# Denominators' transfers and first-layer stores on GpSimd's queue, values loaded last, the first layer a unit later, and another order of the last layer's left factors

## The chip, the cores and the metric

One core of a Trainium2 chip runs the whole program. Its engines are TensorE (PE, the matmuls; PEld is its weight loads), VectorE (DVE), ScalarE (ACT), GpSimd (POOL) and SyncE (SP, which here only issues transfers). Each engine takes its instructions strictly in order. The metric is the device time of one execution in microseconds: 926.24 us before, the median of three runs (923.36 to 926.26).

## The reference

A linear attention and two feed-forward layers, on 4 batches x 576 tokens and 8 heads of 64:

```python
proj = x @ w_phi;  proj -= max(abs(proj), axis=-1)
phi(x) = concat([exp(proj), exp(-proj)])             # 256 features, for q and for k
kv = k_p^T @ v;  z = sum_s k_p
attn = (q_p @ kv) / (q_p @ z + 1e-6)                 # numerators by denominators
h = max(attn @ w1, attn @ w2, attn @ w3)             # 2304 x 768, first layer
y = h @ w_out                                        # 2304 x 512, second layer
g = relu(y @ w_in) + alpha * min(y @ w_in, 0)        # 2304 x 2048, third layer
out = g @ w_out2                                     # 2304 x 512, last layer
```

## The kernel before

Matmuls run in a rounded 32-bit format. To keep accuracy a value x is split into a rounded part (line 68, ACT) and the rest (line 74, a subtraction, mostly on DVE), and a product is taken as three products of parts (`three`). A float32 matmul, used in the first two batches of the attention, is recorded as two.

**Attention.** The loop over `pairs` takes two heads at a time, 16 pairs, 4 to a batch. `load_pair` loads keys (k), values (v), the last 64 tokens of both (t) and queries (q), a pair ahead. `keys` projects (pj), takes the maximum (line 204, DVE), exponentiates on ACT and sums into kvp; `queries`, which runs a pair later, projects, transposes (pt), exponentiates and multiplies by kv, which leaves numerators and denominators in `nd` (line 335, ACT). The 18 pieces of w1, w2, w3 arrive as 64-bit floats (`fetch`, line 173) and are rebuilt on DVE and ACT (`split_w123`) in the first eight pairs.

**The denominators.** At the end of `queries` two small transfers spread the denominators over the partitions (dc, line 366), one moves the second head's numerators (line 367), DVE adds the epsilon and takes reciprocals (368, 369), one transfer writes them to HBM (r_d, line 371), and four read them back, broadcast, into two tiles xr (line 378). A product (line 380), a rounding and a subtraction make the first layer's input (xh, xl). For batch 0 these three run on POOL, later on DVE and ACT. All the transfers stand in SP's queue, between the loads and most of the first layer's stores.

**First layer.** A unit (`layer1`) is 36 matmuls for 288 tokens x 128 outputs: three sums (`p_814`, `p_827`, `p_840` for the first unit), each over four pairs' tiles. Its maximum goes to h_d (line 417; in the last batch from POOL). Units stand three to a pair behind the attention of the next batch, moved by `LAG`. They need all four pairs of their batch.

**Second and third layer.** `load_h` reads h_d back through tiles borrowed from several pools, and the second layer's results (yo, two buffers shared with ho) are stored from ACT's queue and read back by `load_y`. `convert` spreads the rebuilding of later weights over the units. The third layer stores g from POOL (line 628).

**Last layer.** `left` makes, for each half of a block of 256 tokens, seven left factors (a Strassen scheme, seven products in place of eight): four sums and differences s (lines 593 to 596), and for each factor a rounding on ACT and a subtraction, in turn on DVE and POOL. A half is 84 matmuls (line 656). The factors are made one half ahead of their use; DVE adds the results (668, 679).

The order within each engine's queue is laid down when the program is built: a scheduler places instructions by the order of the code and the priorities given there (`tc.high_priority`), so that an edit also moves instructions that it doesn't name.

Of the kernel before, what the change touches and what calls it, by code (L numbers as in the profile page):

```python
# [10 lines left out]
F32 = mybir.dt.float32  # L11
# [22 lines left out]
CHUNKS = ((0, 2 * P), (2 * P, S - 2 * P))  # L34
EPS = 1e-6
XBUFS = (6, 6)
LAG = 1
PLAIN = 5
CONVERT_IN = (2, 1, 2, 1, 3, 3, 3, 3)
SOON, NOW, LATER, LAST = 400, 1000, -100, -200  # L40
# [11 lines left out]
def tile_kernel(ctx: ExitStack, tc: tile.TileContext, qT, kT, tails, v, w_phi, w1, w2, w3, w_out, w_in, w_out2, alpha, out):  # L52
# [82 lines left out]
    def load_pair(pair):  # L135

        odd = pair[1] % 2
        tags = ["xh", "rv", "rt", "xl"] if plain(pair) else ["raw", "rv", "rt", "raw"]
        if plain_kv(pair):
            tags[1] = ("vl", "vh")[odd]  # L140
        shapes = ([P, SM], [P, 5, 3, D], [P, 2 * ST], [P, SM])
        for what, tag, shape, src in zip("kvtq", tags, shapes, (kT, v, tails, qT)):
            t = ap.tile(shape, F32, tag=tag, bufs=2 if tag in ("raw", "xh", "xl") else 1, name=what)
            nc.sync.dma_start(t, src[pair])
            raws[pair, what] = t

    def plain(pair):
        return pair[0] * NPAIR + pair[1] < PLAIN

    def plain_kv(pair):  # L150
        return pair[0] < 2
# [161 lines left out]
    def queries(pair):  # L313

        parts = ("q",) if plain_kv(pair) else ("qh", "ql")
        qf = []
        for n, (o, w) in enumerate(CHUNKS):
            qf.append([])
            for x in parts:
                tag = f"qh{n}" if x != "ql" and pair[1] % 2 * len(x) != 1 else f"ql{n}"  # L320
                qf[n].append(ap.tile([P, 2, 2, w], F32 if plain_kv(pair) else F32R, tag=tag, bufs=1, name=x))
        nd = [ap.tile([P, S], F32, tag="nd", bufs=3, name="nd") for _ in range(2)]

        def num(n):
# [12 lines left out]
        def tail():  # L337
            yield 2, (0,), tail_of[pair]

        for g, tiles, pp in chain(project_queries(pair), tail()):  # L340
            o, w = (0, 2 * P, SM)[g], ST if g == 2 else 2 * P
            pt = bank("pn" if pair[0] == 0 and g == 1 else "pt", 1, "pt")
            for i in range(len(tiles)):
                for h in range(2):
                    c = h * len(tiles) * P + i * P
                    nc.tensor.transpose(pt[:, c : c + P], pp[:, 2 * i + h], ident)  # L346
            n = min(g, 1)
            dst = [t[:, :, :, o - CHUNKS[n][0] : o - CHUNKS[n][0] + w] for t in qf[n]]
            if plain_kv(pair):
                e = dst[0]  # L350
            else:
                e = ap.tile([P, 2, 2, 256], F32, tag="qe", bufs=2, name="qe")[:, :, :, :w]
            pv = pt[:, : 256 * len(tiles)].rearrange("p (h s) -> p h s", h=2)[:, :, -w:]
            A.activation(e[:, :, 0], pv, AF.Exp)
            A.activation(e[:, :, 1], pv, AF.Exp, scale=-1.0)
            if not plain_kv(pair):
                (hi_dve if g == 1 else hi_act)(dst[0], e)
                sub(V, dst[1], e, dst[0])
            yield
            if g != 1:  # L360
                num(n)
        yield
        dc = ap.tile([P, S // D], F32, tag="dc", bufs=2, name="dc")
        for h in range(2):
            dr = D * (1 - h)
            nc.sync.dma_start(dc[h * D : (h + 1) * D], nd[h][dr : dr + 1].rearrange("a (p n) -> a p n", p=D))
        nc.sync.dma_start(nd[0][D:], nd[1][D:])
        V.tensor_scalar(dc, dc, EPS, None, op0=ALU.add)
        V.reciprocal(dc, dc)
        rows = r_d[pair[0], pair[1]]  # L370
        nc.sync.dma_start(rows.rearrange("h (p n) -> (h p) n", p=D), dc)
        res = []
        for c in range(2):
            cs = slice(c * CH, (c + 1) * CH)
            xr = raw_tile()
            for h in range(2):
                r = slice(h * D, (h + 1) * D)
                nc.sync.dma_start(xr[r], rows[h : h + 1, cs].to_broadcast([D, CH]))
            e = G if pair[0] == 0 else V
            e.tensor_tensor(xr, nd[0][:, cs], xr, op=ALU.mult)  # L380
            xh, xl = x_tiles(c)
            if pair[0] == 0:
                G.tensor_copy(xh, xr)  # L383
            else:
# [13 lines left out]
    def layer1(b, c, f, x, w, spread=False):  # L398
        pw = []
        for j in range(3):  # L400
            if spread:
                p = bank(("pn", "pt", "kv")[j], 1, "p1")
            else:
                p = bank("p1", 3, "p1")
            ops = []
            for k in range(KT):
                ks = slice(k * P, (k + 1) * P)
                ops += three(w[j][:, 0, ks], w[j][:, 1, ks], *x[k][c])
            products(p[:, :CH], ops)
            pw.append(p)  # L410
        s1 = xp.tile([P, CH], F32, tag="s1", bufs=2, name="s1")
        A.activation(s1, pw[0][:, :CH], AF.Copy)
        V.tensor_tensor(s1, pw[1][:, :CH], s1, op=ALU.max)
        ho = xp.tile([P, CH], F32, tag="ho", bufs=2, name="ho")
        V.tensor_tensor(ho, pw[2][:, :CH], s1, op=ALU.max)  # L415
        o = b * S + c * CH
        (nc.gpsimd if b == B - 1 else nc.sync).dma_start(h_d[f, :, o : o + CH], ho)  # L417

    pairs = [(b, pr) for b in range(B) for pr in range(NPAIR)]
    xs = {b: [] for b in range(B)}  # L420
# [94 lines left out]

    def load_h(c, k):
        hh, hl = x_tiles(max(c % 2, k // XBUFS[0]))
        pool, tag, bufs = ((xp, "xr", 3), (xp, "xr", 3), (xp, "s1", 2), (gp, "neg", 2))[(2 * c + k) % 4]
        if c == 0:
            pool, tag, bufs = xp, "xr", 3  # L520
        hr = pool.tile([P, CH], F32, tag=tag, bufs=bufs, name="hr")
        nc.sync.dma_start(hr, h_d[k, :, c * CH : (c + 1) * CH])
        hi_act(hh, hr)
        sub(V, hl, hr, hh)
        hs[c, k] = (hh, hl)
# [22 lines left out]
    for c in range(2 * B):  # L548
        t0 = c * CH
        p2 = [bank(*ab, "p2") for ab in SETS[c % 2]]  # L550
        if c + 1 < 2 * B:
            for k in range(NF1):
                load_h(c + 1, k)
        for m in range(KT):
            ms = slice(m * P, (m + 1) * P)
            ops = []
            for k in range(NF1):
                ops += three(wo[k][:, 0, ms], wo[k][:, 1, ms], *hs[c, k])
            products(p2[m][:, :CH], ops)
            yo = xp.tile([P, CH], F32, tag="ho", bufs=2, name="yo")  # L560
            A.activation(yo, p2[m][:, :CH], AF.Copy)
            nc.scalar.dma_start(y_d[m, :, t0 : t0 + CH], yo)
        convert(2)
# [18 lines left out]
    def left(block, half):  # L582

        ready[block, half] = res = {}
        a = []
        for kh in range(2):
            t = ap4.tile([P, 4, 2 * T], F32, tag="a", bufs=4, name="a")
            r = slice(kh * 8 + half * 4, kh * 8 + half * 4 + 4)
            nc.sync.dma_start(t, g_d[r, :, block * 2 * T : (block + 1) * 2 * T].rearrange("f p n -> p f n"))
            a.append(t)  # L590
        (a00, a10), (a01, a11) = ((t[:, :, :T], t[:, :, T:]) for t in a)
        s1, s2, s3, s4 = (ap4.tile([P, 4, T], F32, tag="s", bufs=4, name="s") for _ in range(4))
        V.tensor_tensor(s3, a00, a10, op=ALU.subtract)
        V.tensor_tensor(s1, a10, a11, op=ALU.add)
        V.tensor_tensor(s2, s1, a00, op=ALU.subtract)
        V.tensor_tensor(s4, a01, s2, op=ALU.subtract)  # L596
# [140 lines left out]
```

## Time and profile before

| | |
|---|---|
| median of three runs | 926.24 us (923.36 to 926.26) |
| the profiled execution | 925.09 us, of which its span 923.3 us |
| PE busy | 899.8 us, 97% |
| DVE busy | 642.5 us, 70% |
| ACT busy | 468.2 us, 51% |
| POOL busy | 173.5 us, 19% |

The profile is one execution. Times in its rows are from the span's start. A row of the windows gives each engine's busy time in a stretch and, behind an x, its instructions; PE's busy time contains matmuls that wait in its pipeline, so that the count of matmuls of one kind in 20 us says more than the busy share. A row of the timeline ends with the idle time of the engine before it and what ended it. "SPq" is SP's queue: a row there is an issue, not the transfer's own time.

### The profile page before, as it was taken

To read this page: it belongs to the slowest core of one execution; us is meant where nothing else is said; L and a number is where in the kernel's file an instruction comes from. 1 tells how busy PE (TensorE), PEld (TensorE's weight loads), DVE (VectorE), ACT (ScalarE), POOL (GpSimd) and SP (SyncE) were. 2 spreads that over 40 slices of the span, in tenths; PEclk is the share of its full clock that TensorE was granted. 3 is DMA by queue.
4 is the path that set the end of the run, shared out by engine and by line. 5 is a ranking of instruction groups with operands and counts; after the bars stand their busy time and mean duration, and the time that the engine had idled before them with its cause. 6 is when DMAs were issued, how large, how long until landed. Compare 5 with 4: busy or idle time off the path is not lost.

```text
span 923.3 us, 18029 instructions
## 1 busy us (share of the span) xinstructions
PE 899.8 (97%) x6689; PEld 876.6 (95%) x6689; DVE 642.5 (70%) x1239; ACT 468.2 (51%) x1084; POOL 173.5 (19%) x221
## 2 busy tenths in 40 slices
PE   8987999999999999999999999999999998999998
PEld 7866899999999999999999999999999998999998
DVE  6998556788887632889889294447443598878881
ACT  5867556777777521444466363335333353444440
POOL 0032100000000000001000023333333363444440
PEclk9999999999999999999999999999999999999999
DMA  9664323222331112766678555445542345443421
GB/s 318 195 193 143 84 59 81 74 80 82 104 95 44 31 58 65 225 184 213 203 231 248 185 171 167 131 147 175 193 149 100 111 116 156 135 141 116 138 69 46
DMA packets 83159, 125.98 MB, mean 136 GB/s; under 512 B 14208, under 2 KB 61952, under 8 KB 83072
## 3 DMA queue, kind: packets, MB, share of 16 engines
q1 hardware_dynamic: 71744, 99.47, 36.4%
q0 software_dynamic: 6720, 20.65, 6.2%
q10 hardware_dynamic: 4608, 4.72, 1.5%
q8 instruction: 52, 0.85, 0.4%
q14 instruction: 35, 0.29, 0.1%
HBM read 86.91 MB, written 35.46 MB: 133 GB/s over the span
## 4 chain that ended last, share of the span: by engine, by line
PE 73%; DVE 11%; DMA 8%; issue 3%; ACT 2%; SPq 0%; POOL 0%; ACTq 0%; DVEq 0%; POOLq 0%
PE p L253 43%; PE acc L656 12%; PE kvp L284 6%; PE pn L253 5%; PE pj L253 5%; DVE o L74 2%; DMA st<-in_w_out 2%; DMA y_d<-yo 2%; PE pt L346 2%; DMA hr<-h_d 1%; DVE wt L87 1%; DVE wt L89 1%; ACT o L68 1%; DVE xl L74 1%; DVE s L596 1%
## 5 line engine op out<-in xcount | busy, mean ns | idle before, releaser
L253 PE MATMUL p<-xh,w123t 128*128 128x288 f32 x1152 | 242.3, 298 | 3.2 <-POOL xh L383 3.1
L253 PE MATMUL p<-xh,wi 128*128 128x288 f32 x1024 | 203.9, 296 | 1.2 <-DVE g L627 1.2
L253 PEld LDWEIGHTS p<-xh,w123t 128*128 128x128 f32 x1152 | 187.1, 188 | 4.8 <-POOL xh L383 3.5
L656 PE MATMUL acc<-wq,o 128*128 128x256 f32 x1512 | 182.0, 282 | 3.6 <-DVE o L74 3.2
L656 PEld LDWEIGHTS acc<-wq,o 128*128 128x128 f32 x1512 | 179.9, 190 | 5.6 <-DVE o L74 5.1
L253 PE MATMUL p<-xl,w123t 128*128 128x288 f32 x576 | 171.4, 298 | 0.0
L253 PEld LDWEIGHTS p<-xh,wi 128*128 128x128 f32 x1024 | 163.2, 188 | 1.5 <-DVE g L627 1.5
L253 PE MATMUL p<-xl,wi 128*128 128x288 f32 x512 | 149.5, 293 | 0.0
L253 PEld LDWEIGHTS p<-xl,w123t 128*128 128x128 f32 x576 | 108.2, 188 | 0.6
L628 POOL DMA_DIRECT2D g_d<-g x128 | 69.5, 544 | 208.5 <-DVE g L627 204.6
L627 DVE SCALAR_TENSOR_TENSOR g<-neg,al,p 128x288 f32<-128x288 f32 x128 | 64.3, 511 | 63.7 <-ACT neg L625 63.3
L253 PEld LDWEIGHTS p<-xl,wi 128*128 128x128 f32 x512 | 97.0, 190 | 0.0
L625 ACT ACTIVATE neg<-p 128x288 f32<-128x288 f32 x128 | 51.2, 407 | 84.9 <-PE p L253 81.0
L253 PE MATMUL p<-xh,wo 128*128 128x288 f32 x384 | 76.9, 296 | 0.8 <-ACT xh L68 0.7
L417 POOL DMA_DIRECT2D h_d<-ho x12 | 6.7, 555 | 354.7 <-DVE ho L415 354.7
L68 ACT ACTIVATE o<-s 128x512 fp32r<-128x512 f32 x72 | 44.3, 629 | 55.1 <-PE acc L656 29.6
L74 DVE TENSOR_TENSOR xl<-xr,xh 128x288 fp32r<-128x288 f32 x88 | 38.8, 455 | 37.2 <-ACT xh L68 32.2
L68 ACT ACTIVATE xh<-xr 128x288 fp32r<-128x288 f32 x88 | 37.8, 444 | 49.5 <-DMA xr<-y_d 34.3
L253 PEld LDWEIGHTS p<-xh,wo 128*128 128x128 f32 x384 | 61.1, 188 | 1.3 <-ACT xh L68 1.3
L74 POOL TENSOR_TENSOR o<-s,o 128x512 fp32r<-128x512 f32 x34 | 49.3, 1453 | 65.1 <-ACT o L68 65.1
L204 DVE TENSOR_REDUCE mx<-pj 128x4 f32<-128x512 f32 (+1 forms) x80 | 49.8, 627 | 10.6 <-PE pj L253 10.5
L253 PE MATMUL p<-xl,wo 128*128 128x288 f32 x192 | 56.3, 293 | 0.5 <-DVE xl L74 0.3
(138 smaller groups left out, 1632.3 us busy)
## 6 DMA issues: line engine op xcount, KB each, us to landing
g_d<-g POOLq DMA_DIRECT2D x128, 144.0 KB, 2.1
a<-g_d SPq DMA_DIRECT2D x36, 512.0 KB, 3.8
st<-in_w_out SPq DMA_DIRECT2D x22, 512.0 KB, 4.4
wst<-in_w SPq DMA_DIRECT2D x18, 512.0 KB, 5.6
xr<-y_d SPq DMA_DIRECT2D x64, 144.0 KB, 2.4
st<-in_w_in SPq DMA_DIRECT2D x16, 512.0 KB, 3.8
v<-in_v SPq DMA_DIRECT2D x16, 480.0 KB, 4.2
hr<-h_d SPq DMA_DIRECT2D x48, 144.0 KB, 3.9
```

Source lines behind the costliest of these rows:

```text
L68: A.activation(dst, src, AF.Copy)
L74: eng.tensor_tensor(dst, src, hi.bitcast(F32), op=ALU.subtract)
L87: V.scalar_tensor_tensor(wu, low, 29, wu, op0=ALU.logical_shift_right, op1=ALU.bitwise_or)
L89: V.scalar_tensor_tensor(wu, high, 0xC0000000, wu, op0=ALU.bitwise_and, op1=ALU.bitwise_or)
L204: V.tensor_reduce(mx, pv, axis=AX.X, op=ALU.max, apply_absolute_value=True, negate=True)
L253: nc.tensor.matmul(dst, x, y, start=i == 0, stop=i == len(ops) - 1, **kw)
L284: nc.tensor.matmul(kvp[:, h * 256 : h * 256 + 256], x[:, t, h : h + 2].rearrange("p a d -> p (a d)"), y[:, c], start=first, stop=t == 4 an ...
L346: nc.tensor.transpose(pt[:, c : c + P], pp[:, 2 * i + h], ident)
L625: A.activation(neg, p, AF.Relu, scale=-1.0)
L627: V.scalar_tensor_tensor(g, neg, al[:, f : f + 1], p, op0=ALU.mult, op1=ALU.add)
L628: nc.gpsimd.dma_start(g_d[f, :, c * CH : (c + 1) * CH], g)
L656: nc.tensor.matmul(acc[i], x, y, start=half == 0 and f == 0 and n == 0 and PLACE[i][1] == 0, stop=half == 1 and f == 3 and n == 2, skip_gr ...
```

## The change

```diff
-LAG = 1
+LAG = 2
@@ load_pair
-        for what, tag, shape, src in zip("kvtq", tags, shapes, (kT, v, tails, qT)):
+        for what, tag, shape, src in sorted(zip("kvtq", ...), key=lambda x: ("ktqv" if i_of(pair) else "kvtq").index(x[0])):
@@ queries
-            nc.sync.dma_start(dc[h * D : (h + 1) * D], ...)
-        nc.sync.dma_start(nd[0][D:], nd[1][D:])
+            nc.gpsimd.dma_start(dc[h * D : (h + 1) * D], ...)
+        nc.gpsimd.dma_start(nd[0][D:], nd[1][D:])
-        nc.sync.dma_start(rows.rearrange("h (p n) -> (h p) n", p=D), dc)
+        nc.gpsimd.dma_start(rows.rearrange("h (p n) -> (h p) n", p=D), dc)
-                nc.sync.dma_start(xr[r], rows[h : h + 1, cs].to_broadcast([D, CH]))
-            e = G if pair[0] == 0 else V
+                nc.gpsimd.dma_start(xr[r], rows[h : h + 1, cs].to_broadcast([D, CH]))
+            e = G if i_of(pair) < NPAIR - 1 else V
@@ layer1
-        (nc.gpsimd if b == B - 1 else nc.sync).dma_start(h_d[f, :, o : o + CH], ho)
+        nc.gpsimd.dma_start(h_d[f, :, o : o + CH], ho)
@@ load_h
-        pool, tag, bufs = ((xp, "xr", 3), (xp, "xr", 3), (xp, "s1", 2), (gp, "neg", 2))[(2 * c + k) % 4]
-        if c == 0:
-            pool, tag, bufs = xp, "xr", 3
+        tag, bufs = ("s1", 2) if c and k % 2 else ("xr", 3)
@@ second layer
-            yo = xp.tile([P, CH], F32, tag="ho", bufs=2, name="yo")
+            pool, tag = ((xp, "ho"), (gp, "neg"))[m % 2]
+            yo = pool.tile([P, CH], F32, tag=tag, bufs=2, name="yo")
@@ left
-            t = ap4.tile([P, 4, 2 * T], F32, tag="a", bufs=4, name="a")      # one for each kh
+        a = ap4.tile([P, 2, 4, 2 * T], F32, tag="a", bufs=2, name="a")       # one for both
-        V.tensor_tensor(s3, ...); V.tensor_tensor(s1, ...); V.tensor_tensor(s2, ...); V.tensor_tensor(s4, ...)
-        for n, i in enumerate(ORDER):
             ...
-            sub(G if n % 2 and block + half else V, ov[:, 1], src, ov[:, 0])
+            sub(V, ov[:, 1], src, ov[:, 0])
+        factor(0, a00); s1; s2; yield; factor(5, s2); s3; yield; factor(6, s3); yield; factor(4, s1); yield
+        factor(1, a01); yield; factor(3, a11); s4; yield; factor(2, s4)
```

The last two lines are written short: each s stands for its `V.tensor_tensor`, and `factor` is the body of the old loop.

The first place is TensorE's order just ahead of the first matmul that needs the last pair of batch 0. Before, these rows stand there; `p_814` is the first sum of the first unit, and the last row here is that matmul (the same sum's earlier rows use the other three pairs):

```order
107 L346 MATMUL pt<-ident,pp 128x128 x4
108 L284 MATMUL kvp<-ke,v 128x256 x4
109 L253 MATMUL pn<-q,kvf 128x256 x2
110 L346 MATMUL pt<-ident,ppt 128x128 x2
111 L284 MATMUL kvp<-ke,v 128x256 x2
112 L253 MATMUL p_814<-xh,w123t 128x288
```

With the change, the corresponding rows, again down to that matmul:

```order
111 L287 MATMUL kvp<-ke,v 128x256 x3
112 L256 MATMUL pj<-wph,xhq 128x256
113 L256 MATMUL pj<-wpl,xhq 128x256
114 L256 MATMUL pj<-wph,xlq 128x256
...
118 L287 MATMUL kvp<-ke,v 128x256
119 L256 MATMUL pj<-wph,xhk 128x256
120 L256 MATMUL pj<-wpl,xhk 128x256
121 L256 MATMUL pj<-wph,xlk 128x256
...
125 L256 MATMUL p_814<-xh,w123t 128x288
```

Two groups of six projections (xhq, xlq and xhk, xlk), two kvp and two pn, which stood behind that matmul, now stand ahead of it.

The second place is POOL's queue in batch 0. Before, it holds only the products, roundings (CAST) and subtractions of the pairs:

```order
9 L380 TENSOR_TENSOR xr<-nd,xr 128x288 x2
10 L383 CAST xh<-xr 128x288 x2
11 L74 TENSOR_TENSOR xl<-xr,xh 128x288 x2
12 L380 TENSOR_TENSOR xr<-nd,xr 128x288
13 L383 CAST xh<-xr 128x288
```

With the change, from the third pair's broadcasts to the fourth pair's and beyond (the fourth pair's products are on DVE now):

```order
30 L383 TENSOR_TENSOR xr<-nd,xr 128x288
31 L369 DMA dc<-nd 64x1x9
32 L386 CAST xh<-xr 128x288
33 L369 DMA dc<-nd 64x1x9
34 L383 TENSOR_TENSOR xr<-nd,xr 128x288
35 L74 TENSOR_TENSOR xl<-xr,xh 128x288
36 L370 DMA nd<-nd 64x576
37 L386 CAST xh<-xr 128x288
38 L374 DMA r_d<-dc 128x9
39 L74 TENSOR_TENSOR xl<-xr,xh 128x288
40 L381 DMA xr<-r_d 64x288 x4
42 L420 DMA h_d<-ho 128x288
```

Each pair's eight transfers, and the units' stores, stand between POOL's own products, and SP's queue keeps only loads.

The third place is DVE's queue in the last layer, about one half of a block, in the middle of the layer. Before (o are factors, s the sums):

```order
1079 L593 TENSOR_TENSOR s<-a 128x512
1080 L594 TENSOR_TENSOR s<-a 128x512
1081 L74 TENSOR_TENSOR o<-a,o 128x512
1082 L595 TENSOR_TENSOR s<-s,a 128x512
1083 L74 TENSOR_TENSOR o<-s,o 128x512
1084 L596 TENSOR_TENSOR s<-a,s 128x512
```

With the change:

```order
1095 L602 TENSOR_TENSOR s<-a 128x512
1096 L74 TENSOR_TENSOR o<-s,o 128x512
1097 L603 TENSOR_TENSOR s<-s,a 128x512
1098 L606 TENSOR_TENSOR s<-a 128x512
1099 L74 TENSOR_TENSOR o<-a,o 128x512
1100 L615 TENSOR_TENSOR s<-a,s 128x512
1101 L74 TENSOR_TENSOR o<-s,o 128x512 x2
```

The subtractions that stood in POOL's queue (51 over the layer) are DVE's now, and the factors are spread between the sums.

## Rows read from the trace of the kernel before

**Rows 1.** Page, part 4: shares of the chain that ended last.

```profile
PE 73%; DVE 11%; DMA 8%; issue 3%; ACT 2%; SPq 0%; POOL 0%; ACTq 0%; DVEq 0%; POOLq 0%
```

**Rows 2.** Windows: stretch, length, busy us (x count) by engine, clock, DMA share, GB/s.

```profile
80.00:100.00 20.00, 14.79 (x94) 12.88 (x93) 16.96 (x39) 13.82 (x38) 4.71 (x6) 1.00 0.35 104
...
460.00:480.00 20.00, 19.48 (x143) 18.80 (x143) 17.52 (x37) 13.38 (x32) 0.00 (x0) 1.00 0.73 225
...
500.00:520.00 20.00, 19.22 (x144) 18.77 (x143) 11.20 (x24) 8.06 (x21) 0.00 (x0) 1.00 0.76 239
520.00:540.00 20.00, 18.76 (x142) 18.53 (x141) 11.24 (x25) 12.33 (x30) 1.25 (x2) 1.00 0.47 144
...
580.00:600.00 20.00, 20.00 (x153) 20.00 (x153) 9.31 (x20) 7.58 (x19) 6.21 (x12) 1.00 0.43 135
...
740.00:760.00 20.00, 19.58 (x165) 19.18 (x164) 19.25 (x21) 9.72 (x19) 12.07 (x8) 1.00 0.44 126
760.00:780.00 20.00, 17.13 (x130) 16.72 (x131) 16.05 (x24) 7.83 (x14) 8.25 (x6) 0.91 0.44 132
...
800.00:820.00 20.00, 19.97 (x170) 19.77 (x169) 16.43 (x24) 9.10 (x15) 9.26 (x7) 1.00 0.43 132
```

**Rows 3.** Timeline, 47 to 86 us: start, us, engine, operation; idle before <-releaser.

```profile
47.88 0.28 DVE L368 TENSOR_SCALAR dc<-dc 128x9 f32<-128x9 f32 x1 [2.04 <-DMA dc<-nd]
...
62.71 0.48 PE L253 MATMUL pj<-wraw,k 128*128 128x256 f32 x1 [2.67 <-ACT ke L235]
...
70.68 0.58 SPq L144 DMA_DIRECT2D t<-in_tails  x1
...
73.03 0.83 DVE L71 CAST xht<-t 128x128 fp32r<-128x128 f32 x1 [3.43 <-DMA t<-in_tails]
...
85.53 0.36 PE L253 MATMUL pj<-wph,xht 128*128 128x256 f32 x1 [1.79 <-DVE pp L208]
```

**Rows 4.** Chain in order of time (start, us, what), a stretch of kvp matmuls.

```profile
31.95 1.73 PE kvp L284 x8
```

**Rows 5.** Timeline: the denominators of batch 0's last pair, down to TensorE.

```profile
84.57 0.37 SPq L371 DMA_DIRECT2D r_d<-dc  x1
...
88.06 2.38 SPq L378 DMA_DIRECT2D xr<-r_d  x4
...
91.40 1.59 POOL L380 TENSOR_TENSOR xr<-nd,xr 128x288 f32<-128x288 f32 x1 [12.33 <-DMA xr<-r_d]
...
93.53 0.40 PE L253 MATMUL p<-xh,w123t 128*128 128x288 f32 x1 [3.12 <-POOL xh L383]
```

**Rows 6.** DMA issues (KB, median us to landing); durations min/median/max; a DVE group.

```profile
xr<-r_d SPq DMA_DIRECT2D x64, 72.0 KB, 2.7
h_d<-ho SPq DMA_DIRECT2D x36, 144.0 KB, 2.5
h_d<-ho POOLq DMA_DIRECT2D x12, 144.0 KB, 3.2
...
L628 POOL DMA_DIRECT2D g_d<-g x128: 539/539/867, 538.1 to 735.0; - x128
...
L380 DVE TENSOR_TENSOR xr<-nd,xr 128x288 f32<-128x288 f32 x24 | 11.0, 456 | 25.5 <-DMA xr<-r_d 23.2 <-issue 2.1
```

**Rows 7.** Timeline of the last layer's start.

```profile
737.29 0.69 DVE L74 TENSOR_TENSOR o<-a,o 128x512 fp32r<-128x512 f32 x1 [0.73 <-ACT o L68]
...
742.29 1.74 POOL L74 TENSOR_TENSOR o<-a,o 128x512 fp32r<-128x512 f32 x1
742.80 1.78 DVE L74 TENSOR_TENSOR o<-a,o 128x512 fp32r<-128x512 f32 x1
...
763.35 0.41 DVE L668 TENSOR_TENSOR out<-acc,u 128x256 f32<-128x256 f32 x1
...
764.42 0.58 PE L656 MATMUL acc<-wq,o 128*128 128x256 f32 x1 [2.86 <-DVE o L74]
```

**Rows 8.** Waits: engine, line, releaser, total us, times, longest.

```profile
ACT yo L561 <- DMA y_d<-yo: 19.2, 11, 4.4
```

More of the change, by code (lines that the diff above doesn't have):

```diff
@@ L141, in load_pair @@
         shapes = ([P, SM], [P, 5, 3, D], [P, 2 * ST], [P, SM])
-        for what, tag, shape, src in zip("kvtq", tags, shapes, (kT, v, tails, qT)):
+        for what, tag, shape, src in sorted(zip("kvtq", tags, shapes, (kT, v, tails, qT)), key=lambda x: ("ktqv" if i_of(pair) else "kvtq").index(x[0])):
             t = ap.tile(shape, F32, tag=tag, bufs=2 if tag in ("raw", "xh", "xl") else 1, name=what)
@@ L147, in plain, with i_of @@
     def plain(pair):
-        return pair[0] * NPAIR + pair[1] < PLAIN
+        return i_of(pair) < PLAIN
+    def i_of(pair):
+        return pair[0] * NPAIR + pair[1]
     def plain_kv(pair):
@@ L365, in queries @@
             dr = D * (1 - h)
-            nc.sync.dma_start(dc[h * D : (h + 1) * D], nd[h][dr : dr + 1].rearrange("a (p n) -> a p n", p=D))
-        nc.sync.dma_start(nd[0][D:], nd[1][D:])
+            nc.gpsimd.dma_start(dc[h * D : (h + 1) * D], nd[h][dr : dr + 1].rearrange("a (p n) -> a p n", p=D))
+        nc.gpsimd.dma_start(nd[0][D:], nd[1][D:])
         V.tensor_scalar(dc, dc, EPS, None, op0=ALU.add)
@@ L377, in queries @@
                 r = slice(h * D, (h + 1) * D)
-                nc.sync.dma_start(xr[r], rows[h : h + 1, cs].to_broadcast([D, CH]))
-            e = G if pair[0] == 0 else V
+                nc.gpsimd.dma_start(xr[r], rows[h : h + 1, cs].to_broadcast([D, CH]))
+            e = G if i_of(pair) < NPAIR - 1 else V
             e.tensor_tensor(xr, nd[0][:, cs], xr, op=ALU.mult)
             xh, xl = x_tiles(c)
-            if pair[0] == 0:
+            if e is G:
                 G.tensor_copy(xh, xr)
@@ L517, in load_h @@
         hh, hl = x_tiles(max(c % 2, k // XBUFS[0]))
-        pool, tag, bufs = ((xp, "xr", 3), (xp, "xr", 3), (xp, "s1", 2), (gp, "neg", 2))[(2 * c + k) % 4]
-        if c == 0:
-            pool, tag, bufs = xp, "xr", 3
-        hr = pool.tile([P, CH], F32, tag=tag, bufs=bufs, name="hr")
+        tag, bufs = ("s1", 2) if c and k % 2 else ("xr", 3)
+        hr = xp.tile([P, CH], F32, tag=tag, bufs=bufs, name="hr")
         nc.sync.dma_start(hr, h_d[k, :, c * CH : (c + 1) * CH])
@@ L584, in left, with factor @@
         ready[block, half] = res = {}
-        a = []
+        a = ap4.tile([P, 2, 4, 2 * T], F32, tag="a", bufs=2, name="a")
         for kh in range(2):
-            t = ap4.tile([P, 4, 2 * T], F32, tag="a", bufs=4, name="a")
             r = slice(kh * 8 + half * 4, kh * 8 + half * 4 + 4)
-            nc.sync.dma_start(t, g_d[r, :, block * 2 * T : (block + 1) * 2 * T].rearrange("f p n -> p f n"))
-            a.append(t)
-        (a00, a10), (a01, a11) = ((t[:, :, :T], t[:, :, T:]) for t in a)
+            nc.sync.dma_start(a[:, kh], g_d[r, :, block * 2 * T : (block + 1) * 2 * T].rearrange("f p n -> p f n"))
+        (a00, a10), (a01, a11) = ((a[:, kh, :, :T], a[:, kh, :, T:]) for kh in range(2))
         s1, s2, s3, s4 = (ap4.tile([P, 4, T], F32, tag="s", bufs=4, name="s") for _ in range(4))
[L593 to L596, printed above, removed]
-        for n, i in enumerate(ORDER):
-            src = (a00, a01, s4, a11, s1, s2, s3)[i]
+        def factor(i, src):
             o = op4.tile([P, 2, 512], F32R, name="o") if half else ring2.tile([P, 2, 512], F32R, tag="w", name="o")
@@ L601, in left @@
             hi_act(ov[:, 0], src)
-            sub(G if n % 2 and block + half else V, ov[:, 1], src, ov[:, 0])
+            sub(V, ov[:, 1], src, ov[:, 0])
             res[i] = o
-            yield
+        factor(0, a00)
+        V.tensor_tensor(s1, a10, a11, op=ALU.add)
+        V.tensor_tensor(s2, s1, a00, op=ALU.subtract)
+        yield
+        factor(5, s2)
+        V.tensor_tensor(s3, a00, a10, op=ALU.subtract)
+        yield
+        factor(6, s3)
+        yield
+        factor(4, s1)
+        yield
+        factor(1, a01)
+        yield
+        factor(3, a11)
+        V.tensor_tensor(s4, a01, s2, op=ALU.subtract)
+        yield
+        factor(2, s4)
     V.tensor_scalar(al, al, -1.0, 1.0, op0=ALU.mult, op1=ALU.add)
```

## The prediction

> **What bounds the kernel now.** The first view is the chain of waits on the page: TensorE holds 73% of it and DVE 11% [rows 1]. So the reader should ask where TensorE is not fed, and the view for that is the table by 20 us windows [rows 2]. Its counts matter more than its busy times. In a full window of the third layer TensorE gets through 153 matmuls (580 to 600 us), in the last layer 170 (800 to 820 us), which is 0.131 and 0.118 us each. Three places fall short.
>
> The head: from 80 to 100 us TensorE is busy for 14.79 of 20 us, while DVE has 16.96. The second layer: 143, 144 and 142 matmuls in place of 153 in the windows from 460, 500 and 520 us, so 30 are missing, 30 x 0.131 = 3.9 us. The last layer's start: 165 and 130 in place of 170 from 740 and 760 us, 45 missing, 45 x 0.118 = 5.3 us; the second of these windows also shows a granted clock of 0.91, at the lower level for a part of it, after TensorE stood still.
>
> The third view is the timeline at these places. In the head three gaps of TensorE are long [rows 3, 5]: 2.67 us at 62.71, until ACT has finished the exponentials that read the projection's bank; 1.79 us at 85.53, until DVE has freed such a bank; 3.12 us at 93.53, until batch 0's last pair has reached the first layer. I call the last one the gate: behind it first-layer units fill whatever the attention leaves open. The three make 7.6 us.
>
> DVE itself idles in that stretch for transfers that SP issues: 2.04 us at 47.88 for the denominators (dc) and 3.43 us at 73.03 for the last tokens (t) [rows 3]. That t load went out at 70.68, directly behind broadcasts of reciprocals in SP's queue. The gate's own chain shows the same queue: the write of the reciprocals issues at 84.57, the broadcasts at 88.06, POOL's product begins at 91.40 and takes 1.59 us, and TensorE starts at 93.53 [rows 5].
>
> **The change part by part.** The profiled execution took 925.09 us, 923.3 us span and 1.8 us around it, and lies 1.15 us under the median of 926.24. The sum is made against 925.1.
>
> *The first layer a unit later, and the gate.* The order shows what this and the rescheduling do there: twelve rounded projections, two kvp and two pn now stand ahead of the gate. A rounded matmul of 256 columns costs 0.118 us as in the last layer [rows 2]; a float32 one is two records of 1.73 / 8 = 0.216 us [rows 4]. So 12 x 0.118 + 4 x 2 x 0.216 = 3.1 us of work that was done after the gate covers a wait of 3.12 us. The pair's product also moves from POOL (1.59 us at the gate) to DVE (0.456 us [rows 6]), 1.1 us sooner. I count 3.1 us gained.
>
> *SP's queue without the denominators and stores.* 128 transfers of the denominators and 36 stores leave SP. The t load is then no longer behind a broadcast, and dc no longer behind loads; DVE gets up to 2.04 + 3.43 us back, and the one long gap that ends with DVE (1.79 us) should go. What is late next is DVE's own work, which fills 85% of the window. Counted: 1.8 us. For the gap of 2.67 us the order now puts kv transposes and a pair's kvp sums ahead of that projection, some 2.4 us of matmuls by the same durations; they wait for ACT too, so I count half the gap, 1.4 us.
>
> *What it costs.* DVE takes over two products and two subtractions of the fourth pair, 4 x 0.456 = 1.8 us, on the engine that is busiest there; half of it on the path, 0.9 us. The POOL route of dc, r_d and xr is not in this trace. From below, it costs what SP's does, 2.7 us for a broadcast to land, or less, since POOL's queue has no loads in it; from above, the same store lands in 3.2 us from POOL against 2.5 us from SP [rows 6], 0.7 us more, and three such hops follow each other, 2.1 us. I take nothing, since the gate has about 1.1 us to spare and DVE runs ahead, and keep the 2.1 us for the range. Values loaded last: nothing, since a pair's loads run a pair ahead; in the batches behind the gate TensorE is full.
>
> Head: 3.1 + 1.8 + 1.4 - 0.9 = 5.4 us.
>
> *Second layer.* Results get four buffers where two were. ACT waited 19.2 us in all, 11 times, for the store of an earlier result [rows 8], and it stands ahead of the roundings that TensorE waits for. These waits should go. In return the loads borrow five buffers in place of up to seven, so the sixth load of a step waits for a subtraction of the same step. Of the 3.9 us I count 1.5, between 0 and 3.9.
>
> *Last layer.* Alone, a subtraction of DVE takes 0.69 us; beside one of POOL's (1.74 us) it takes 1.78 us [rows 7]. POOL's subtractions therefore cost DVE more than they take from it. TensorE's wait of 2.86 us at 764.42 ends with such a DVE subtraction. Without POOL's share DVE has per block of 20 us: 8 sums and 14 subtractions x 0.69 = 15.2 us, and seven additions x 0.41 = 2.9 us, 18.1 us. That fits, and the first factor no longer waits for four sums. I count 4.5 of the 5.3 us, with 2 to 5.3 as bounds; the clock's share is in it, since without a wait of 3 us it should not fall. In the steady blocks (170 per window) nothing is to be had.
>
> Sum: 5.4 + 1.5 + 4.5 = 11.4 us; 925.1 - 11.4 = 913.7. With the median 1.15 us over the profile I say 914 us.
>
> **Rivals.** A: POOL's hops are slow. For it: 3.2 us against 2.5 us, and POOL's issues, mostly 539 ns, reach 867 ns [rows 6]. Eight issues a pair at 0.33 us more and three hops at 0.7 us make 4.7 us at the gate. The head then gives 0.7 us: 918.4 us. Against it: the median issue is the shortest one.
> The Trainium skill (SBUF — State Buffer, "Who interferes with whom") states a rule for this: while DVE runs a cast or tensor_scalar in its two-port mode, GpSimd can't write the descriptors of its own transfers and waits until DVE is done. By that rule these eight issues would each wait for whatever such instruction DVE is in, which leads to A; the trace agrees only weakly, with 0.33 us at the longest of 128 issues.
>
> B: the head is bound by DVE's amount of work, not by SP's order, so that the change doesn't do what it says there. For it: 16.96 of 20 us. Against it: DVE's idle times end with SP's transfers. Then the last layer alone gains: 925.1 - 4.5 = 920.6 us.
>
> C: DVE becomes the bound of the last layer. 18.1 of 20 us leaves 1.9 us a block, and each subtraction waits for ACT's rounding. At 0.5 us lost in each of nine blocks the 4.5 us are given back: 918.2 us.
>
> D, slower: POOL's single queue holds up the first layer. A store stands behind broadcasts that wait for a landing. Its sources have two buffers, which last for two units, at least 2 x 36 x 0.131 = 9.4 us and longer by the attention's matmuls between them; when POOL holds a store beyond that, DVE stops at its next maximum and everything behind it. A pair's issues (8 x 0.54) and two landings (2 x 3.2) make 10.7 us if nothing lies between them. If so TensorE might lose 1 us in each of 12 pairs; the head and the second layer then gain nothing, and the time is 925.1 - 4.5 + 12 = 932.6 us. Against it: a pair brings three units and its own attention, so that the buffers last well beyond 9.4 us.
>
> **How the numbers follow.** Forecast 0.55, A 0.18, B 0.10, C 0.10, D 0.07. About 0.3%, 2.8 us, is what a measurement here can tell from none, so "faster" means under 923.5 us: nearly all of the forecast and most of A, B and C, together 0.87; the same 0.06; slower 0.07, D. All three places at their best give 7.6 + 3.9 + 5.3 = 16.8 us, 908.3; the short gaps of the head that I did not count bring the lower end to 907. A, B and C lie at 918 to 921, so the upper end is 922. The forecast's own range is 909 to 918.
>
> **What would show it.** Right: in the head t and dc no longer end long idle times of DVE, and the gate is not the longest gap; POOL's dc, r_d and xr land within 3.2 us; from 740 to 780 us the windows hold nearly 170 matmuls at a clock of 1.00, and DVE's subtractions stay near 0.69 us; ACT no longer waits for yo's store. Wrong: the gate still with a gap of 3 us and POOL issues near 0.9 us (A); DVE gapless in the head with TensorE waiting (B); under 168 matmuls in the last layer's later windows (C); DVE's second maximum waiting for the store of its buffer (D).

## The result, and the profile after

The changed kernel takes 917.29 us, the median of eight runs (913.99 to 921.0), against 925.18 us for the kernel before in eight runs beside them: a ratio of 0.9915, 95% interval 0.9894 to 0.9936. Its profiled execution took 915.64 us, span 913.9 us, 9.4 us less than the span before. The direction was forecast and the time lies 3.3 us above the forecast. But the gain did not come from where I put it.

The windows of the changed kernel, to be read against [rows 2]; columns: stretch, its length, busy us (x count) of PE, PEld, DVE, ACT and POOL, granted clock, DMA share, GB/s.

```profile
40.00:60.00 20.00, 18.04 (x87) 14.37 (x86) 19.57 (x34) 13.32 (x28) 12.36 (x21) 1.00 0.67 207
60.00:80.00 20.00, 17.84 (x93) 14.01 (x91) 19.10 (x38) 15.02 (x40) 10.40 (x17) 1.00 0.58 168
80.00:100.00 20.00, 17.37 (x91) 14.12 (x90) 18.88 (x44) 15.48 (x45) 4.89 (x9) 0.91 0.32 95
460.00:480.00 20.00, 19.01 (x144) 18.70 (x142) 18.11 (x37) 12.50 (x30) 0.00 (x0) 1.00 0.76 239
480.00:500.00 20.00, 19.23 (x131) 19.02 (x132) 17.48 (x37) 12.29 (x30) 0.00 (x0) 0.91 0.72 232
...
740.00:760.00 20.00, 20.00 (x172) 20.00 (x172) 17.97 (x33) 9.10 (x16) 0.00 (x0) 1.00 0.44 139
760.00:780.00 20.00, 20.00 (x172) 20.00 (x172) 16.11 (x29) 8.54 (x16) 0.00 (x0) 1.00 0.40 126
```

The last layer is full: 172 matmuls from its first window on, where 165 and 130 stood, and 172 is more than the 170 that I had taken for full. The second layer still falls short: 144 and 131 in place of 153. In the head DVE, which idled for transfers before, is now busy for 57.6 of 60 us (51.1 before), and TensorE still isn't fed.

To compare many kernels I use one number per stretch, worked out from the records of TensorE's matmuls: the time from the start of each matmul to the start of the next, less what its shape takes back to back in full stretches (0.1175 us for a rounded one of 256 columns, 0.133 for 288, 0.146 for 320; float32 records by shape). The sum is what TensorE lost there, waits and lower clock together; a few tenths either way are rounding. One profiled execution each, us:

```
kernel                        0-105  105-440  440-545  545-725  725-end
before                         18.0      2.0      3.9     -0.3      7.8
after (the change)             16.7      1.3      4.2      0.1      0.0
e1 before, new factors         17.9      3.1      1.6     -0.3      0.0
e2 after, old factors          19.0      1.5      3.6     -0.1      6.9
e3 after, POOL's share back    18.0      1.6      3.4     -0.2     20.2
e4 after, old order, DVE       19.6      2.3      4.0      0.0      0.1
e5 after, denominators on SP   14.9      1.8      7.5      0.6      0.0
e6 after, pair 3 on GpSimd     17.2      1.5      3.6      0.6      0.1
e7 after, other CONVERT_IN     21.3      1.9      3.8      0.3      0.0
e8 after, old second layer     19.3      2.5      5.2     -0.2      0.0
e9 after, light conversion      7.3      1.3      2.4      0.2      0.0
e10 after, six load buffers    19.1      1.4      0.2      0.2      0.0
e11 = e5 and e10               16.2      3.1      0.6     -0.3      0.0
e12 = e11, conversions later   10.3      1.3     -0.4     -0.2      0.0
```

Between before and after the last layer gives 7.8 us, the head 1.3 us, and the second layer takes 0.3 us. The table also shows how far executions of the same head differ. In e2, e3, e4, e7, e8 and e10 every engine has the changed kernel's instructions in the changed kernel's order up to 370 us. They lost 18.0 to 21.3 us in the head; with the 16.7 us of the changed kernel itself the mean of the seven is 19.0. The kernel before and e1, which share the old head, lost 18.0 and 17.9 us. So the 1.3 us can't be told from nothing, nor can the 0.3 us: the kernel before and e1 have the same second layer too, and lost 3.9 and 1.6 us there.

In this execution of the head the long waits did go. This is the view of TensorE's waits of the changed kernel from 20 to 105 us (what waited, for what; us in total, times, longest).

```profile
PE pj L256 <- ACT ke L238: 1.2, 1, 1.2
PE kvt L301 <- ACT kvs L298: 1.2, 1, 1.2
PE kvp L287 <- ACT kvf L304: 1.0, 1, 1.0
PE pt L349 <- ACT q L358: 1.0, 2, 0.6
PE pt L349 <- DVE pp L211: 0.8, 1, 0.8
```

None of the three gaps of [rows 3, 5] is there. (The other six executions of this head lack the gate's gap and the one of 2.67 us as well, but each has a new one of 3.1 to 3.3 us at 48 to 50 us, which is shown with e7.) In their place stand eight of 0.4 to 1.2 us (the five longest rows are shown), and after two of them, at 83 and 85 us, TensorE is granted the lower of its two levels (1.2 in place of 2.4 GHz) for a part of the window, which is the 0.91 above: 0.09 x 20 = 1.8 us of full speed.

Where such a short gap comes from is seen in the timeline of the changed kernel around the first of them (start, us, engine, operation; idle before, releaser).

```profile
79.49 0.68 DVE L207 TENSOR_REDUCE mx<-pj 128x4 f32<-128x512 f32 x1
...
80.09 0.41 DVE L85 TENSOR_SCALAR wt<-wt 128x512 uint32<-128x512 uint32 x1
...
80.43 0.64 DVE L83 TENSOR_SCALAR wt<-wt 128x512 f32<-128x512 f32 x1
...
80.99 0.16 DVE L235 TENSOR_SCALAR my<-mx 128x4 f32<-128x4 f32 x1
...
81.18 0.37 ACT L238 ACTIVATE ke<-pj,my 128x128 f32<-128x128 f32 x1 [0.49 <-DVE my L235]
...
83.15 0.39 PE L256 MATMUL pj<-wph,xhk 128*128 128x256 f32 x1 [1.21 <-ACT ke L238]
```

Between the maximum (mx) and its negative (my, 0.16 us) two steps of a weight's conversion stand in DVE's order. ACT waits for my, and TensorE for ACT.

### The profile page after: what moved, and what is told of

Read it like the earlier page. It is cut to its first block, busy times and chain, and to the rows that moved or that the text cites. A ratio compares the mean times of both kernels' runs of the same rounds, so it can differ in the third digit from the quotient of the medians.

```text
span 913.9 us, 17994 instructions
## 1 busy us (share of the span) xinstructions
PE 897.4 (98%) x6689; PEld 876.1 (96%) x6689; DVE 643.9 (70%) x1294; ACT 470.4 (51%) x1086; POOL 179.6 (20%) x328
## 4 chain that ended last, share of the span: by engine, by line
PE 45%; DMA 6%; DVE 3%; ACT 1%; issue 1%; DVEq 0%; ACTq 0%; SPq 0%
PE p L256 26%; PE acc L669 19%; DMA st<-in_w_in 4%; DMA xr<-y_d 1%; DMA hr<-h_d 1%; DVE wt L89 1%; DMA st<-in_w_out 1%; ACT wt L81 1%; DVE xl L74 0%; DVE wt L87 0%; DVE wt L83 0%; ACT xh L68 0%; DVE wi L74 0%; DVE wq L74 0%; ACT wq L68 0%
## 5 line engine op out<-in xcount | busy, mean ns | idle before, releaser
L669 PE MATMUL acc<-wq,o 128*128 128x256 f32 x1512 | 177.8, 280 | 0.0
L669 PEld LDWEIGHTS acc<-wq,o 128*128 128x128 f32 x1512 | 177.7, 188 | 0.0
L420 POOL DMA_DIRECT2D h_d<-ho x48 | 26.8, 558 | 137.9 <-DVE ho L418 132.2
L68 ACT ACTIVATE o<-a 128x512 fp32r<-128x512 f32 x54 | 33.7, 629 | 37.6 <-PE acc L669 25.5
```

The source lines that it names most:

```text
L68: A.activation(dst, src, AF.Copy)
L420: nc.gpsimd.dma_start(h_d[f, :, o : o + CH], ho)
L669: nc.tensor.matmul(acc[i], x, y, start=half == 0 and f == 0 and n == 0 and PLACE[i][1] == 0, stop=half == 1 and f == 3 and n == 2, skip_gr ...
```

## The experiments

### Which stage gives the gain

```diff
e1: before, with left() of the changed kernel
e2: after, with left() of the kernel before
```

> The kernel before with one part of the change alone: the last layer's left factors in the new order and without GpSimd's share; head and second layer stay as before. Theory L (nearly all of the gain is the last layer's: TensorE lost 7.6 us there before and nothing after): 7 to 8 us less than before, ratio 0.992, so about as fast as the whole change; 172 matmuls in each window of the last layer, no fall of the clock at its start. Rival H (my sum: the last layer 4.5 us, head and second layer 6.9 us): 4.5 us less, ratio 0.995, clearly slower than the whole change.

> The changed kernel with the last layer's left factors put back to the old order and with GpSimd's share: what is left is the change in head and second layer. Theory L: no more than 1 us less than before, ratio 0.999 (0.997 to 1.001), with 130 and 165 matmuls again in the last layer's first windows. Rival H: 6.9 us less, ratio 0.9925.

e1: 916.5 us, ratio to before 0.9916 (0.9895 to 0.9936). e2: 924.91 us, 0.9998 (0.9981 to 1.0015). So the new left factors alone are as fast as the whole change, and all the rest of it together is worth nothing that can be measured. Theory L holds.

### Contention or order in the last layer

```diff
e3: after
-            sub(V, ov[:, 1], src, ov[:, 0])
+            sub(G if len(res) % 2 and block + half else V, ov[:, 1], src, ov[:, 0])
e4: after, with left() of before
-            sub(G if n % 2 and block + half else V, ov[:, 1], src, ov[:, 0])
+            sub(V, ov[:, 1], src, ov[:, 0])
```

> The changed kernel with the new order of the left factors, but GpSimd takes every second subtraction again (all but the first block's first half). If the contention of the two engines is the cause (theory C1): DVE's subtractions beside POOL's go to 1.7 us, TensorE waits again, 3 to 7 us more than the changed kernel. If the order with the first factor ahead of the sums is the cause (theory C2): within 1 us of the changed kernel.

> The changed kernel with the old order of the left factors (four sums first, then seven factors, a tile for each half of the operands) but all subtractions on DVE. Theory C1 (contention): within 1 us of the changed kernel. Theory C2 (order): 3 to 7 us more, with the wait of TensorE at the last layer's first factor of a half still there.

e3: 937.22 us, 1.0153 (1.0125 to 1.0181), slower than before. e4: 918.73 us, 0.994 (0.9918 to 0.9962), with nothing lost in the last layer. So taking GpSimd out is the whole of it, and the order by itself gave nothing; with GpSimd's share the new order is much worse than the old: 20 us above the changed kernel, where 3 to 7 were expected. Groups of e3 from 740 to 900 us (line, engine, operation, shapes, count; busy us, mean ns; idle before, releaser):

```profile
L669 PE MATMUL acc<-wq,o 128*128 128x256 f32 x1205 | 148.3, 286 | 12.2 <-DVE o L74 11.4 <-ACT o L68 0.8
...
L74 POOL TENSOR_TENSOR o<-s,o 128x512 fp32r<-128x512 f32 x29 | 44.1, 1532 | 79.5 <-ACT o L68 77.3 <-PE acc L669 2.1
...
L74 DVE TENSOR_TENSOR o<-s,o 128x512 fp32r<-128x512 f32 x30 | 29.7, 989 | 5.8 <-ACT o L68 5.8
...
L615 DVE TENSOR_TENSOR s<-a,s 128x512 f32<-128x512 f32 x15 | 18.7, 1247 | 0.2
L602 DVE TENSOR_TENSOR s<-a 128x512 f32<-128x512 f32 x14 | 16.2, 1155 | 29.5 <-DMA a<-g_d 29.5
```

The same groups of the changed kernel:

```profile
L669 PE MATMUL acc<-wq,o 128*128 128x256 f32 x1364 | 160.4, 280 | 0.0
...
L74 DVE TENSOR_TENSOR o<-s,o 128x512 fp32r<-128x512 f32 x66 | 43.9, 685 | 1.4 <-ACT o L68 1.1
...
L602 DVE TENSOR_TENSOR s<-a 128x512 f32<-128x512 f32 x16 | 11.0, 690 | 12.9 <-DMA a<-g_d 12.9
L615 DVE TENSOR_TENSOR s<-a,s 128x512 f32<-128x512 f32 x16 | 11.0, 687 | 0.2
```

A sum of 0.69 us takes 1.16 to 1.25 us beside GpSimd's subtractions. In the new order the sums stand between the factors, and TensorE waits for the next one. The loads of a come later too, 29.5 us of DVE's idle time against 12.9; which of the two makes the new order so much worse with GpSimd's share is not shown.

### The head: transfers and the gate

```diff
e5: after, in queries()
-            nc.gpsimd.dma_start(dc, nd, r_d, xr ...)
+            nc.sync.dma_start(dc, nd, r_d, xr ...)
e6: after
-            e = G if i_of(pair) < NPAIR - 1 else V
+            e = G if pair[0] == 0 else V
```

> The changed kernel with the denominators' transfers (dc, nd, r_d, xr) issued by SP again; the first layer's stores stay with GpSimd. Theory P (GpSimd's issues stretch DVE's work, and DVE's work is the bound of the head): DVE's TENSOR_SCALAR at L83 goes from 685 ns back to about 500 between 40 and 100 us, DVE is busy about 53 of these 60 us in place of 57.5, and the time is that of the changed kernel or up to 3 us less. Rival Q (SP's order is the bound, as I forecast): DVE waits again for the last tokens and the denominators, 2 to 4 us more.

> The changed kernel with the fourth pair's products, roundings and subtractions on GpSimd again. Theory G (the gate hides nothing of them, as I forecast): TensorE stands before the first layer again, 1 to 3 us more. Rival W (DVE's amount of work is the bound and the gate lies behind other work now): DVE has 1.8 us less to do, 0 to 2 us less.

e5: 917.62 us, 0.9928 (0.9901 to 0.9956). e6: 918.15 us, 0.9938 (0.9915 to 0.996). Neither can be told from the changed kernel. So the queue from which the denominators go out is not what the head waits for (Q falls): e11, whose head has e5's order, shows DVE waiting 3.2 us for t and 2.0 us for dc again, and TensorE lost 16.2 us there, not more. And the gate doesn't wait for the fourth pair's product even where GpSimd makes it (G falls): e6 has no such wait of TensorE. (The 7.5 us of e5 from 440 to 545 us hold a gap of 2.2 us in the second layer and a stretch at the lower clock behind it; the edit does not touch that place.)

P holds in its size, and in its cause only in part. L83 took 562 ns in e5 against 685 ns, and DVE was busy for 53.8 of the 60 us, but the timeline of the changed kernel shows what stretches L83:

```profile
50.73 0.56 POOL L374 DMA_DIRECT2D r_d<-dc  x1 [1.81 <-DVE dc L372]
...
50.91 1.51 DVE L83 TENSOR_SCALAR wt<-wt 128x512 f32<-128x512 f32 x1
...
51.31 0.81 POOL L74 TENSOR_TENSOR xl<-xr,xh 128x288 fp32r<-128x288 f32 x1
...
52.73 2.18 POOL L381 DMA_DIRECT2D xr<-r_d  x4 [0.60 <-DMA r_d<-dc]
...
53.87 0.41 DVE L85 TENSOR_SCALAR wt<-wt 128x512 uint32<-128x512 uint32 x1
...
57.10 1.51 DVE L83 TENSOR_SCALAR wt<-wt 128x512 f32<-128x512 f32 x1
...
57.51 0.82 POOL L383 TENSOR_TENSOR xr<-nd,xr 128x288 f32<-128x288 f32 x1
```

A TENSOR_SCALAR of DVE takes 0.41 us beside four issues of GpSimd, and 1.51 us when a product or subtraction of GpSimd falls into it; it then ends 0.3 us after GpSimd's instruction. So GpSimd's arithmetic, which the change leaves there for three pairs, is what stretches it; issues alone don't (five cases, 0.41 to 0.42 us). Both of these instructions of GpSimd begin right behind an issue, so whether the issue adds something is open; in e7 an L83 beside two products and no issue took 1.86 us.

### The head: DVE's amount of work

```diff
e7: after
-CONVERT_IN = (2, 1, 2, 1, 3, 3, 3, 3)
+CONVERT_IN = (1, 1, 1, 0, 4, 4, 4, 3)
e9: after, in split_w123(): only ACT's first step of from_f64
-        yield from from_f64(st, wt)
+        yield from list(zip(range(1), from_f64(st, wt)))
```

> The changed kernel with three conversions of first-layer weights (five DVE instructions, some 3.3 us of DVE's time each) moved from the first four pairs to behind the gate, where DVE is busy for about 11 of 20 us: CONVERT_IN 1, 1, 1, 0, 4, 4, 4, 3 in place of 2, 1, 2, 1, 3, 3, 3, 3. Theory W (DVE's amount of work is the head's bound): DVE is no longer full from 40 to 100 us, TensorE loses 4 to 8 us less there, 910 to 913 us. Rival (the head is bound by TensorE's chain through ACT or by transfers): within 1 us of the changed kernel.

> The changed kernel without four of the five DVE instructions of each first-layer weight's conversion (L83, L85, L87, L89), so that those weights are wrong and DVE has some 2.6 us less to do for each of the 11 or 12 conversions between 40 and 100 us, 30 of the 57.5 us. Theory W (DVE's amount of work is what the head waits for): TensorE loses under 12 us from 0 to 105 us in place of 16.7, and the time is 4 to 8 us less than the changed kernel. Rival K (the head is bound by the steps that follow one another within a pair, projection, maximum, exponential, sums, each on another engine): 15 us or more are still lost, and the time is within 2 us of the changed kernel.

e7: 918.07 us, 0.9941 (0.992 to 0.9962). This looked like a verdict against W, but the edit had not done what it meant to: its trace has as many conversions from 40 to 100 us as the changed kernel's, 12, since the scheduler fills DVE's free places ahead of time with whatever is ready. In fact every engine has the changed kernel's instructions in the same order throughout, so that e7 says nothing on W and is a second profile of the changed kernel. This is the conversions' group in e7, and its timeline at the new gap:

```profile
L87 DVE SCALAR_TENSOR_TENSOR wt<-wst,wt 128x512 uint32<-128x512 uint32 x12 | 10.1, 839 | 0.1
...
46.03 2.43 DVE L74 TENSOR_TENSOR w123t<-wt,w123t 128x512 fp32r<-128x512 f32 x1
46.36 0.80 POOL L383 TENSOR_TENSOR xr<-nd,xr 128x288 f32<-128x288 f32 x1
47.11 0.79 POOL L74 TENSOR_TENSOR xl<-xr,xh 128x288 fp32r<-128x288 f32 x1
48.98 0.68 DVE L211 TENSOR_TENSOR pp<-pj,mx 128x512 f32<-128x512 f32 x1
...
49.71 0.80 PE L256 MATMUL pj<-wraw,k 128*128 128x256 f32 x1 [3.14 <-DVE pp L211]
```

A subtraction of a weight's conversion, 0.69 us alone, takes 2.43 us beside a product and a subtraction of GpSimd; pp stands behind it in DVE's order, and TensorE waits 3.14 us for pp. It is the same in the other five executions (2.41 to 2.43 us, a gap of 3.1 to 3.3 us). In the changed kernel's own profile the same subtraction stood at 43.72 us, before these two began (45.49 and 46.24 us), and took 0.69 us. In these six executions the head thus lost at this place about what it had gained at the gate.

e9 leaves out four of DVE's five steps of each conversion: 905.14 us, 0.9797 (0.9777 to 0.9818), which is more than W expected. TensorE loses 0.6 us from 40 to 105 us in place of 11.9, with no gap of a quarter of a us. Its windows:

```profile
40.00:60.00 20.00, 20.00 (x100) 16.91 (x99) 15.52 (x29) 19.65 (x47) 9.56 (x16) 1.00 0.68 209
60.00:80.00 20.00, 20.00 (x115) 17.50 (x114) 9.63 (x26) 13.87 (x44) 13.79 (x24) 1.00 0.40 113
80.00:100.00 20.00, 19.98 (x124) 17.76 (x123) 11.62 (x27) 14.12 (x44) 6.75 (x14) 1.00 0.28 82
```

So the head waits for DVE, and what keeps DVE is its weight conversions. Rival K falls. The scheduler laid the queues down anew for e9 (TensorE's order differs from 18 us on), so the amount of the conversions and their place in DVE's order are not told apart by it.

### The second layer

```diff
e8: after, with load_h and yo of before
e10: after
-        tag, bufs = ("s1", 2) if c and k % 2 else ("xr", 3)
+        pool, tag, bufs = ((xp, "xr", 3), (xp, "s1", 2), (gp, "neg", 2))[(0, 1, 0, 1, 0, 2)[k] if c else 0]
-            pool, tag = ((xp, "ho"), (gp, "neg"))[m % 2]
+            pool, tag = ((xp, "ho"), (gp, "neg"))[m == 1]
```

> The changed kernel with the second layer's buffers as before (results in the two buffers of ho, loads in up to seven). Theory S (the change gives ACT's wait for a store away and gets a later load for it): TensorE's loss from 440 to 540 us goes from 4.3 to between 1.6 and 3.9 us, 0.5 to 2 us less than the changed kernel. Rival (my term): ACT waits for the stores again, 1.5 us more.

> The changed kernel with a buffer for each of the six loads of a step of the second layer (the sixth takes one of neg's two, and only one of a step's four results goes there), so that no load waits for a subtraction of its own step. Theory S2 (the sixth load's wait is what the change put in place of ACT's wait for a store): TensorE loses under 2 us from 440 to 545 us in place of 4.2, and the time is 1.5 to 3 us less than the changed kernel. Rival (the loads are late because of the memory traffic, whichever buffer they have): 3 us or more lost there, the time within 1 us of the changed kernel.

e8: 919.46 us, 0.9956 (0.9936 to 0.9976): not the gain that theory S wanted. In its profile ACT waits 15.3 us for stores again. It lies 0.4% above the changed kernel, and the two intervals meet at 0.9936, so whether the change gained something here stays open. e10: 913.33 us, 0.9884 (0.9862 to 0.9906), 0.2 us lost in the second layer. The time's interval still overlaps the changed kernel's. ACT's waits from 440 to 545 us, first of the changed kernel:

```profile
ACT xh L68 <- DMA hr<-h_d: 16.2, 11, 4.2
ACT wt L81 <- DMA st<-in_w_out: 13.7, 7, 2.8
```

and of e10:

```profile
ACT wt L81 <- DMA st<-in_w_out: 10.1, 5, 2.4
...
ACT xh L68 <- DMA hr<-h_d: 4.4, 6, 1.2
ACT yo L563 <- DMA y_d<-yo: 3.2, 3, 1.9
```

The change took the wait for a store [rows 8] away and put one for a load in its place. With a buffer for each load both are small. The rival (traffic) falls: the DMA engines are busier in e10 than in the changed kernel (0.85 against 0.72 from 480 to 500 us) and the loads still come in time.

### Two candidates

```diff
e11: e5 and e10 together
e12: e11, and
-CONVERT_IN = (2, 1, 2, 1, 3, 3, 3, 3)
+CONVERT_IN = (2, 1, 3, 3, 3, 3, 3)
-    with tc.high_priority(offset=LAST if i < NPAIR - 1 else 0):
+    with tc.high_priority(offset=LAST):
+    zeros[f] = ap.tile([P, 1], F32, ...)      # once for each weight block f > 0
+    A.activation(zeros[f], nds[f][1][:, S - 1 : S], AF.Abs, scale=0.0)
-        A.activation(w, high.bitcast(F32), AF.Abs)
+        A.activation(w, high.bitcast(F32), AF.Abs, bias=zeros[f])
```

> A candidate for a faster kernel: the changed one with the denominators' transfers on SP (in the profile with these TensorE lost 14.9 us in the head in place of 16.7) and a buffer for each of the second layer's six loads. If both gains add up: 1.7 and 2 us less than the changed kernel, 913 to 914 us. If the stalls only change places: within 1 us of the changed kernel.

> A candidate for a faster kernel, and the move that the kernel with CONVERT_IN 1, 1, 1, 0, 4, 4, 4, 3 did not make: the kernel with the denominators on SP and six load buffers, in which the conversions of the first-layer weights from the second block on are held back until a column of a given pair's numerators exists (ACT's first step adds zero times that column), so that about 6 in place of 12 stand between 40 and 100 us in DVE's order. Theory W (the head waits for DVE, which is full of conversions): TensorE loses under 10 us from 0 to 105 us in place of 16.2, 906 to 909 us. Rival (the conversions then press on the stretch from 100 to 200 us, where DVE has 11 to 16 of 20 us to do already): what the head gains is lost there, 911 us or more.

e11: 912.22 us, 0.9869 (0.9846 to 0.9892), 1.1 us below e10 with intervals that overlap. e12: 905.48 us, 0.9798 (0.9774 to 0.9822), the fastest, and all of the reference is computed. A conversion cannot be placed before the numerators of a given pair, because its first step adds a zero that is made from them. Windows of e12:

```profile
40.00:60.00 20.00, 19.53 (x99) 15.98 (x97) 16.98 (x32) 16.11 (x39) 9.09 (x12) 1.00 0.48 152
60.00:80.00 20.00, 19.18 (x108) 17.11 (x108) 18.30 (x40) 15.94 (x43) 5.32 (x6) 1.00 0.62 178
80.00:100.00 20.00, 16.99 (x107) 14.97 (x106) 15.73 (x39) 15.62 (x41) 0.71 (x1) 1.00 0.54 159
100.00:120.00 20.00, 20.00 (x134) 18.82 (x133) 14.57 (x33) 11.07 (x30) 1.08 (x2) 1.00 0.39 113
```

The six conversions that I expected from 40 to 100 us are ten. They went from elsewhere: summed over their instructions, DVE spends 39.2 us on conversions up to 100 us in place of e11's 52.2 (56.9 in the changed kernel), and of these 13 us 9.5 lie between 20 and 40 us and 4.2 between 40 and 60 us, where the held-back ones would have stood (0.7 us came back behind 60 us). The attention's steps on DVE then run ahead, and TensorE loses 6.0 us from 40 to 105 us in place of e11's 11.4 (10.3 from the start, just over the 10 that W named). Behind 100 us the conversions cost TensorE nothing (1.3 us lost from 105 to 440 us, e11 3.1): the rival falls, and W stands for a kernel that leaves nothing out. What is left to gain there is e12's 4.1 us from 80 to 105 us, and was not tried further; nor was taking GpSimd's arithmetic out of the first three pairs.

## Why the prediction was right, and where its sum was not

**Last layer, 4.5 us forecast, 7.8 us measured** (7.4 us in e1 by its medians, 923.87 to 916.5). The mechanism was right: DVE's subtractions take 685 ns once POOL has none. Mis-sized was the bound. "In the steady blocks (170 per window) nothing is to be had" took the fullest row of the kernel before for a full one. Full is 172 to 173, and behind 785 us the kernel before had lost 1.8 us. The rest is the start, where the wait and the lower clock behind it went together. (That the clock falls only behind a wait of 3 us does not hold: in the head it fell behind gaps of 1.21 and 1.00 us.) My reason that "the first factor no longer waits for four sums" carried nothing (e4).

**Head, 5.4 us forecast, 1.3 us between two profiles, none by e2 or by all executions of this head.** Three things happened as forecast. The gate's wait of 3.12 us is gone; DVE waits 0.8 us for t and 0.3 us for dc; the wait of 2.67 us is gone. The step that failed is "DVE gets up to 2.04 + 3.43 us back", for which I counted 1.8 us on the path, with "late next is DVE's own work" named and not priced. DVE's work went from 51.1 to 57.6 us: 1.8 us for the fourth pair as counted, a conversion more, and the stretching beside POOL. I had read that stretching in the last layer [rows 7] and priced it only there; in the head the gap of 3.1 us of e7 and its like stands behind it. That conversions stand between the attention's steps is seen in the timeline above, and that they are what the head waits for in e9 and e12. That is rival B, to which I gave 0.10, and with the 7.8 us measured in the last layer its sum is 925.1 - 7.8 = 917.3 us, the measured time; "DVE's idle times end with SP's transfers" was a true reading and no argument against it, since an engine may idle in one place and be late in the next.

**Second layer, 1.5 us forecast, -0.3 us between two profiles.** The waits for the stores went as forecast. "The sixth load waits for a subtraction of the same step" was named as well, and its price left no gain that can be told from none; e10 shows it by removing it.

**The rivals.** A: false as priced. From POOL a broadcast lands in 2.7 us, as it did from SP, and r_d in 1.9 us; only dc is slower, 2.4 us against 1.8. Issues and landings of the changed kernel, and behind the gap dc's of the kernel before (queue, operation, count; KB, median us to landing):

```profile
xr<-r_d POOLq DMA_DIRECT2D x64, 72.0 KB, 2.7
...
dc<-nd POOLq DMA_DIRECT2D x32, 2.2 KB, 2.4
r_d<-dc POOLq DMA_DIRECT2D x16, 4.5 KB, 1.9
...
dc<-nd SPq DMA_DIRECT2D x32, 2.2 KB, 1.8
```

The broadcasts' issues took 533 ns each on average. Of all 304 issues of GpSimd in the changed kernel 13 took over 600 ns, each of them beside a TENSOR_SCALAR or CAST of DVE, and 12 ended 0.10 to 0.12 us after it. The longest (start, us, engine, operation; idle before, releaser):

```profile
260.68 1.00 POOL L369 DMA_DIRECT2D dc<-nd  x1 [3.59 <-ACT s L415]
260.89 0.68 DVE L71 CAST qh<-qe 128x1024 fp32r<-128x1024 f32 x1
```

Counted against 540 ns, the 13 cost 2.7 us over the whole kernel, and the four of them in the head 0.7 us, where A had 4.7 us at the gate. The rule of the Trainium skill that spoke for A (SBUF — State Buffer, "Who interferes with whom") says that GpSimd waits with its descriptors while DVE is in its two-port mode. The trace agrees that GpSimd waits (which mode DVE was in it doesn't show); the wait was small. The same section says that two engines that share this port exclude each other, and that a DVE instruction with two SBUF inputs contends with a GpSimd instruction that reads SBUF. That the trace agrees with: 0.69 us became 1.16 to 1.25 us in e3 and 2.43 us in e7. C: false, nothing is lost at 16 to 18 of 20 us of DVE. D: false, from 105 to 440 us TensorE lost 1.3 us, not more than before (2.0 us).

That the total came near is luck: two terms were too large by 4.1 and 1.8 us and one too small by 3.3 us, and by e1 and e2 the last layer gave all of the gain.

## What to carry to other kernels

Two elementwise engines that read the same memory are not two engines: price the slower one by what it takes from the faster, and try the kernel with the faster alone. Where a scheduler fills an engine's free places with work that is not yet due, an idle time that you remove can be filled again; hold that work back by a dependency, not by a number that the scheduler may pass over. And a full window is the fullest that any version of the kernel shows, not the fullest of the version at hand. And one profile is one execution: the same instructions in the same order lost 16.7 us of TensorE's time in the head in one and 21.3 us in another.

## What the runs showed of the hardware that was not expected

A TENSOR_SCALAR of DVE on 128x512 took 0.41 us, also beside transfers issued by GpSimd. When a GpSimd TENSOR_TENSOR of 0.81 us began 0.4 us after it, it took 1.51 us, and when one was under way as it began, 0.96 us; in all four such cases of the changed kernel's head it ended 0.28 to 0.30 us after GpSimd's instruction. The other way round, 13 of the 28 issues of GpSimd that stood beside a TENSOR_SCALAR or CAST of DVE took over 600 ns; 12 of them ended 0.10 to 0.12 us after DVE's instruction, and the longest took 1.00 us in place of 0.53.
